# Seven products from the second tile on, earlier sums of weights on GpSimd, and two copies on ScalarE, in a fused attention and feed-forward kernel

## Chip, cores and metric

One core of one Trainium2 chip. The metric is the device time of one execution in microseconds (us); "span" is the time from the first to the last instruction in the trace of one execution, and is about 1.8 us shorter. All runs compared here are of the fast state (single runs without a group are marked so); lower is better.

## What the kernel computes

Attention with keys and values pooled by 8, then a feed-forward layer with the gate `h * cos(h)`:

```python
# q, k, v: (8, 8, 576, 64) float32;  w_in: (512, 2048);  w_out: (2048, 512)
k_p = k.reshape(B, H, Sp, 8, D).mean(axis=3)
v_p = v.reshape(B, H, Sp, 8, D).mean(axis=3)
scores = q @ k_p.T / sqrt(D)
attn = softmax(scores)
x = (attn @ v_p) -> (4608, 512)          # tokens x heads*D
h = x @ w_in
out = (h * cos(h)) @ w_out               # float32
```

The 4608 tokens are cut into nine tiles of 512. Per tile: the *up projection* (64 matmuls of 512 columns, in eight steps of eight; each step ends in a cosine on ScalarE and a product on VectorE, and the products make up `g`), then the *down projection*. Between these matmuls the attention of the next batch is done: scores, exponentials, values, normalisation. GpSimd sums keys and values of the batch after that ("pooling").

## The kernel before: what the change touches

The down projection has two forms. The plain one has 64 matmuls of 512 columns. The other is a 2x2 block product in Winograd's form with seven block products in place of eight: 7 x 16 matmuls of 256 columns. It needs sums of blocks of `g` (`g1` to `g4`, per tile) and of `w_out` (`w2` to `w4`, once). The kernel before uses it from the third tile on (`FIRST = 2`); the sum that product 3 needs is written over half of `w_out` itself, which is only possible after the last plain tile.

```python
FIRST = 2
def put_weights(i, eng, k=None):              # w3, w2, w4: halves of the block sums
    ...
def put_first_weights(i):                     # in place, after tile 1
    w = w_out_sb[i]
    nc.vector.tensor_tensor(out=w[:, :, HM:], in0=w[:, :, HM:], in1=w[:, :, 0:HM], op=SUB)

def put_g12(i): ...                           # VectorE: g1 and g2, half i
def put_g3(i): ...                            # VectorE: g3, half i
def put_g4(i): ...                            # VectorE: g4, half i

for t in range(NT):                           # tiles
    for n, fp in enumerate(up_order(t)):      # eight steps of the up projection
        up_mm(t, fp, ...)                     # matmuls
        up_g(t, fp, ...)                      # cosine on ScalarE, product on VectorE
        if t >= FIRST and 3 <= n < 6:
            (put_g12, put_g3, put_g4)[n - 3](0)
        if t == 1 and 3 <= n < 6:
            put_weights(1, nc.vector, n - 3)
    ...
    if t < FIRST:
        ...                                   # plain down projection with attention between
        if t + 1 == FIRST:
            for i in range(2): put_first_weights(i)
    else:
        product(0); scores_of(u0, u1, u2)     # u2 needs the bank of the eighth up step
        product(1)
        put_g12(1); reads[0](); put_g3(1); reads[1](); put_g4(1)   # reads[0]: the p1 copy
        values(u0); product(2); reads[2](); muls()
        values(u1); product(3); reads[3](); muls()
        values(u2); product(4); reads[4](); muls()
        scores_of(ur, u3)                     # u3 needs the bank that u1's muls() frees
        product(5, ...); ...; product(6); reads[6]()
    ...
    load_kv(b + 1, "k"); load_q(b + 1); load_kv(b + 1, "v")        # loads issued by GpSimd
    if t == 0: put_weights(0, nc.gpsimd)
    pool_add(b + 1, "k"); pool_add(b + 1, "v")                     # GpSimd
```

The softmax here doesn't subtract the row's maximum and nothing guards it: scores larger than these inputs give would overflow.

## Time and profile before

| | kernel before |
|---|---|
| median of 3 runs | 294.95 us (294.61 to 295.21) |
| profiled execution | 296.27 us, span 294.5 us |
| TensorE busy | 96% of the span, granted clock 0.999 |
| tile 0 (down part), 1, 2, 3 | 19.37, 31.60, 31.90, 29.93 us |
| tiles 7 and 8 with the end | 27.46 and 31.30 us |

A tile is counted from its first up matmul to that of the next. The lines for tiles 1 to 3 are quoted in the prediction; those for tiles 7 and 8 have the same columns (stretch and its length, busy time of TensorE, weight loads, VectorE, ScalarE and GpSimd, granted clock, DMA share, GB/s):

```profile
235.74:263.20 27.46, 26.70 (x193) 17.55 (x193) 21.44 (x28) 14.82 (x17) 0.00 (x0) 1.00 0.17 39
263.20:294.50 31.30, 26.42 (x176) 17.11 (x175) 20.38 (x32) 8.96 (x9) 0.00 (x0) 0.99 0.30 68
```

### The profile page before, as it was taken

Reading aid. Unit: us, or ns where it says so; the run is one execution under the profiler, and the core shown is the slowest. Engines: PE = TensorE matmul, PEld = TensorE weight load, DVE = VectorE, ACT = ScalarE, POOL = GpSimd, SP = SyncE. Lnnn points to the kernel's source line nnn. Section 1 sums busy time; section 2 is a strip of 40 time slices with the busy share of each in tenths; the row PEclk is TensorE's granted clock in tenths of the full one; section 3 lists DMA queues with packets and bytes.
Section 4 is the critical chain, followed back from the end, with each engine's and each line's share of the span. In section 5 each row is a group of like instructions: output and inputs, shape, how many; then the busy total and the mean of one; then the engine's idle time right before and its main releaser. Section 6 shows DMA issues by size and latency. Waiting matters only on the chain. (4 is left out here: it accounts for less than half of the span.)

```text
span 294.5 us, 5317 instructions
## 1 busy us (share of the span) xinstructions
PE 282.1 (96%) x2096; PEld 174.0 (59%) x2120; DVE 226.6 (77%) x306; ACT 206.4 (70%) x261; POOL 148.4 (50%) x144
## 2 busy tenths in 40 slices
PE   8899999999999899999999999999999999999984
PEld 3545544444544587458745874588458844774673
DVE  5558547595489998799879887998798879846972
ACT  3786897469767688679967997699769976336500
POOL 8563079993995299536983599349900000000000
PEclk9999999999999999999999999999999999999999
DMA  7999999629817961969185929691840060005014
GB/s 163 205 207 206 207 205 204 139 52 148 168 37 137 139 104 26 200 89 163 19 182 89 169 45 195 92 174 28 173 73 2 4 142 0 2 21 122 2 36 107
DMA packets 44488, 32.95 MB, mean 112 GB/s; under 512 B 22192, under 2 KB 40112, under 8 KB 44464
## 3 DMA queue, kind: packets, MB, share of 16 engines
q0 software_dynamic: 19744, 18.07, 39.2%
q1 hardware_dynamic: 24080, 14.03, 22.2%
q10 hardware_dynamic: 640, 0.52, 0.7%
q8 instruction: 16, 0.26, 0.3%
q14 instruction: 8, 0.07, 0.1%
HBM read 36.70 MB, written 9.44 MB: 157 GB/s over the span
## 5 line engine op out<-in xcount | busy, mean ns | idle before, releaser
L317 PE MATMUL bank<-xT,w_in_sb 128*128 128x512 bf16 x503 | 114.7, 379 | 1.8 <-DVE g_sb L331 0.9
L327 ACT ACTIVATE cos<-bank,half_pi 128x1024 f32<-128x1024 f32 x65 | 71.4, 1113 | 48.5 <-PE bank L317 45.2
L317 PEld LDWEIGHTS <-w_in_sb 128*128 128x128 bf16 x576 | 56.0, 98 | 67.2 <-issue 1.5
L331 DVE TENSOR_TENSOR g_sb<-bank,cos 128x1024 bf16<-128x1024 f32 x65 | 78.4, 1220 | 22.1 <-ACT cos L327 22.0
L151 POOL TENSOR_TENSOR half_sums<-kv_st 72x512 f32<-72x512 bf16 x48 | 56.9, 1212 | 27.3 <-DMA kv_st<-in_k_dram 26.8
L262 DVE TENSOR_TENSOR xT<-bank,inv 64x512 bf16<-64x512 f32 (+1 forms) x72 | 45.3, 629 | 17.9 <-ACT inv L258 16.9
L257 ACT ACTIVATE inv<-bank 64x512 f32<-64x512 f32 (+1 forms) x72 | 39.1, 544 | 12.4 <-PE bank L251 11.2
L402 PEld LDWEIGHTS <-g 128*128 128x128 bf16 x448 | 42.9, 98 | 8.2 <-issue 3.3
L229 ACT ACTIVATE ex<-bank 72x1024 bf16<-72x1024 f32 (+1 forms) x40 | 35.1, 928 | 3.2 <-PE bank L222 3.0
L402 PEld LDWEIGHTS <-g_sb 128*128 128x128 bf16 x336 | 32.1, 98 | 6.9 <-issue 1.0
L153 POOL TENSOR_TENSOR half_sums<-half_sums 72x512 f32<-72x512 f32 x24 | 30.4, 1284 | 0.0
L334 PE MATMUL obank<-w_out_sb,g_sb 128*128 128x512 bf16 x123 | 29.9, 379 | 0.3 <-issue 0.2
L402 PE MATMUL obank<-w,g 128*128 128x256 bf16 x224 | 26.9, 272 | 1.7 <-DVE p_sb L416 1.6
L402 PE MATMUL obank<-w_out_sb,g_sb 128*128 128x256 bf16 x208 | 25.1, 273 | 0.3 <-DVE g_sb L331 0.3
L402 PE MATMUL obank<-w_out_sb,g 128*128 128x256 bf16 x192 | 24.8, 273 | 0.0
L258 ACT ACTIVATE inv<-inv 128x512 f32<-128x512 f32 (+1 forms) x36 | 21.0, 583 | 1.1
L251 PE MATMUL bank<-ex,vz 72*128 72x256 bf16 (+1 forms) x176 | 20.0, 243 | 0.0
L334 PEld LDWEIGHTS <-g_sb 128*128 128x128 bf16 x128 | 11.8, 97 | 12.5 <-issue 1.0
L251 PEld LDWEIGHTS <-vz 72*128 72x128 bf16 x176 | 13.7, 97 | 4.4 <-DVE xT L262 0.5
L156 POOL TENSOR_TENSOR kp<-half_sums 72x512 bf16<-72x512 f32 x12 | 15.0, 1270 | 0.5
L222 PE MATMUL bank<-qT,kk 64*72 64x256 bf16 (+1 forms) x192 | 13.2, 251 | 1.5 <-DVE g_sb L331 0.6
L402 PE MATMUL obank<-w,g_sb 128*128 128x256 bf16 x112 | 13.4, 273 | 0.0
(83 smaller groups left out, 253.6 us busy)
## 6 DMA issues: line engine op xcount, KB each, us to landing
out_dram<-o_two SPq DMA_DIRECT2D x64, 128.0 KB, 2.4
kv_st<-in_v_dram POOLq DMA_DIRECT2D x8, 576.0 KB, 13.6
kv_st<-in_k_dram POOLq DMA_DIRECT2D x7, 576.0 KB, 7.8
q_b<-in_q_dram POOLq DMA_DIRECT2D x6, 576.0 KB, 9.9
w_in_sb<-in_moe_w_in_dram POOLq DMA_DIRECT2D x4, 512.0 KB, 13.1
w_out_sb<-in_moe_w_out_dram POOLq DMA_DIRECT2D x4, 512.0 KB, 18.5
q_b<-in_q_dram POOLq DMA_DIRECT2D x4, 288.0 KB, 11.7
g_sb<-in_k_dram SPq DMA_DIRECT2D x1, 576.0 KB, 3.7
```

Source lines behind the costliest of these rows:

```text
L151: add(out=s[:, h:h + 2], in0=x[:, h:h + 2, 0:4, :], in1=x[:, h:h + 2, 4:8, :], op=ADD)
L153: add(out=s[:, h:h + 4, 0:2, :], in0=s[:, h:h + 4, 0:2, :], in1=s[:, h:h + 4, 2:4, :], op=ADD)
L229: nc.scalar.activation(out=ex[:, 0:nh * n].rearrange("p (a n) -> p a n", a=2), in_=pair[:Sp, :, 0:nh * n // 2], func=ACTF.Exp, scale=scale ...
L251: nc.tensor.matmul(pair[:, hp, (i // 2) * n:(i // 2 + 1) * n], lhsT=vz[b % 2][:, pj, 2 * hp:2 * hp + 2, :].rearrange("p a d -> p (a d)"), ...
L257: nc.scalar.activation(out=inv[half[1 - hp]], in_=pair[half[1 - hp], hp, 0:w], func=ACTF.Ln)
L258: nc.scalar.activation(out=inv, in_=inv, func=ACTF.Exp, scale=-1.0)
L262: nc.vector.tensor_mul(out=x_out(b, u, half[hp]), in0=cols(pair[half[hp], hp, :], u), in1=cols(inv[half[1 - hp]], u))
L317: nc.tensor.matmul(h[j] if h is obanks else h[:, j, :], lhsT=w_in_sb[fc // 4][:, ki, (fc % 4) * 128:(fc % 4 + 1) * 128], rhs=xT[:, ki, t * ...
L327: nc.scalar.activation(out=c, in_=ps, func=ACTF.Sin, bias=half_pi[:, :1])
L331: nc.vector.tensor_mul(out=o, in0=ps, in1=c)
L334: nc.tensor.matmul(o, lhsT=g_sb[:, fc, ms * 128:(ms + 1) * 128], rhs=w_out_sb[fc // 4][:, fc % 4, :], start=(fc == 0), stop=(fc == FFCH - 1))
L402: mms.append(lambda bank=bank, first=first, g=g, w=w, fc=fc, p=p: nc.tensor.matmul(bank[p], lhsT=g(fc, p), rhs=w(fc), start=(first and fc ...
```

## The change

Its intent: gain the eighth product in tile 1 as well. The block sums must then exist before tile 1's down projection, so `w1` gets its own buffer (paid for by one `o_two` buffer), GpSimd makes four half sums ahead of pooling, VectorE four in tile 0, and of the four pieces of `w_out` (0 to 3) the first of the second row block, piece 2, is loaded one place earlier. In tile 1 the sums of `g` are issued later than elsewhere. In the last two tiles the p1 copy goes to ScalarE.

```diff
-    FIRST = 2
+    FIRST = 1
-    w2, w3, w4 = [... for k in range(2, 5)]
+    w1, w2, w3, w4 = [... for k in range(1, 5)]
-        o = msb.tile([128, 2, d_model], FP32, name="o_two", tag="o_two", bufs=3)[:, 0]
+        o = msb.tile([128, 2, d_model], FP32, name="o_two", tag="o_two", bufs=2)[:, 0]
-    def put_first_weights(i): ...                       # removed
+    def put_weights(i, eng, ks=(1, 3, 2, 4)):           # w1 = b12 - b11 is new
-            (Bb, True, part(g1), of(w_out_sb[0:2], 1)),
+            (Bb, True, part(g1), of(w1)),
-                    nc.vector.tensor_copy(out=out[:, p, m], in_=ps)
+                    (nc.scalar.copy if t >= B - 1 else nc.vector.tensor_copy)(out=out[:, p, m], in_=ps)
-    for cg in range(1, 4):
+    for cg in (2, 1, 3):
         load_w_out(cg)
-            if t >= FIRST and 3 <= n < 6:
+            if t == 1 and n == 6:
+                put_g12(0)
+            if t > 1 and 3 <= n < 6:
                 (put_g12, put_g3, put_g4)[n - 3](0)
-            if t == 1 and 3 <= n < 6:
-                put_weights(1, nc.vector, n - 3)
-            mms = [... for cg in range(4) ...]           # tile 0
+            mms = [... for cg in (0, 2, 1, 3) ...]
... (the plain form of tile 1 with its attention is removed)
+                if n == 4:                               # tile 0, matmul number
+                    put_weights(0, nc.vector, (1,))
+                elif n == 36:
+                    put_weights(1, nc.vector, (3,))
+            put_weights(1, nc.vector, (2, 4))
-            put_g3(1)
+            for i in range(0 if t == 1 else 1, 2):
+                put_g3(i)
             reads[1]()
-            put_g4(1)
+            for i in range(0 if t == 1 else 1, 2):
+                put_g4(i)
-                put_weights(0, nc.gpsimd)
+                put_weights(0, nc.gpsimd, (3, 2, 4))
+                put_weights(1, nc.gpsimd, (1,))
```

More of the change, by code (lines that the diff above doesn't have):

```diff
@@ L71 @@
     g1, g2, g3, g4 = [wpool.tile([128, HF, HT], BF16, name=f"g{i}") for i in range(1, 5)]
-    w2, w3, w4 = [[wpool.tile([128, 4, HM], BF16, name=f"w{k}{i}") for i in range(2)] for k in range(2, 5)]
+    w1, w2, w3, w4 = [[wpool.tile([128, 4, HM], BF16, name=f"w{k}{i}") for i in range(2)] for k in range(1, 5)]
     SpA = -(-Sp // 16) * 16
@@ L343, in down_out @@
             nc.sync.dma_start(out=rows_of[b_, ORDER[pos]], in_=o[rows])
-    def put_weights(i, eng, k=None):
-        vec = eng.tensor_tensor
+    def put_weights(i, eng, ks=(1, 3, 2, 4)):
         (b11, b12), (b21, b22) = [(w[:, :, 0:HM], w[:, :, HM:]) for w in (w_out_sb[i], w_out_sb[i + 2])]
-        for n, (w, x, y, op) in enumerate(((w3, b22, b12, SUB), (w2, w3[i], b11, ADD), (w4, b21, w2[i], SUB))):
-            if k in (None, n):
-                vec(out=w[i], in0=x, in1=y, op=op)
-    def put_first_weights(i):
-        w = w_out_sb[i]
-        nc.vector.tensor_tensor(out=w[:, :, HM:], in0=w[:, :, HM:], in1=w[:, :, 0:HM], op=SUB)
+        for k in ks:
+            out, x, y, op = {1: (w1, b12, b11, SUB), 3: (w3, b22, b12, SUB), 2: (w2, w3[i], b11, ADD),
+                             4: (w4, b21, w2[i], SUB)}[k]
+            eng.tensor_tensor(out=out[i], in0=x, in1=y, op=op)
     def g_part(f, t, f0, f1):
@@ L407, in down_products @@
         p1, v16, q15 = [msb.tile([128, 2, HM], FP32, name=n, tag=n, bufs=1) for n in ("p1_sb", "v_sb", "q_sb")]
-        o1, o2 = [msb.tile([128, 2, d_model], FP32, name="o_two", tag="o_two", bufs=3) for _ in range(2)]
+        o1, o2 = [msb.tile([128, 2, d_model], FP32, name="o_two", tag="o_two", bufs=2) for _ in range(2)]
         m1, m2 = slice(0, HM), slice(HM, d_model)
@@ L560 @@
         if t == 0:
-            mms = [(ms, fc) for hm in range(2) for cg in range(4) for ms in range(2 * hm, 2 * hm + 2)
+            mms = [(ms, fc) for hm in range(2) for cg in (0, 2, 1, 3) for ms in range(2 * hm, 2 * hm + 2)
                    for fc in range(4 * cg, 4 * cg + 4)]
@@ L580 @@
                         (32, lambda: later.pop()()), (32, V_(2, 2)), (40, V_(3, 0))]
-        elif t < FIRST:
-            us = BY_TOKENS
-            def scores_of(*parts):
-                def go():
-                    for f in scores_mm, scores_exp:
-                        for b_, u, bank in parts:
-                            f(b_, u, banks[bank])
-                return go
-            fill = [(4, scores_of((b, us[0], 2), (b, us[1], 0))), (14, V_(0, 1, later)), (16, lambda: later.pop()()),
-                    (19, V_(1, 2)), (35, scores_of((b, us[2], 0), (b, us[3], 1), (t, REST, 2))),
-                    (38, V_(2, 0)), (43, lambda: values(t, REST, banks[1])), (46, V_(3, 2))]
         if t < FIRST:
@@ L603 @@
                     down_out(t, ms, obanks[ms % 2])
-            if t + 1 == FIRST:
-                for i in range(2):
-                    put_first_weights(i)
+                if n == 4:
[3 more added lines that the diff above has]
+            put_weights(1, nc.vector, (2, 4))
         else:
```

## The prediction

> **What bounds the kernel now.** I read the page first, then the timelines of TensorE, VectorE, GpSimd and ScalarE, cut at the starts of the nine tiles of 512 tokens, then the busy times by stretch. The page says who fills the span:
>
> ```profile
> span 294.5 us, 5317 instructions
> PE 282.1 (96%) x2096; PEld 174.0 (59%) x2120; DVE 226.6 (77%) x306; ACT 206.4 (70%) x261; POOL 148.4 (50%) x144
> ```
>
> TensorE (PE) is busy 96% of the time at a granted clock of 0.999. So a change pays only if it takes away work of TensorE or one of its few gaps. The table by stretch (TensorE, weight loads, VectorE, ScalarE, GpSimd) shows tile 1, tile 2 and tile 3, cut where each tile's first up-projection matmul starts:
>
> ```profile
> 52.52:84.12 31.60, 31.21 (x175) 15.14 (x177) 19.14 (x24) 23.21 (x30) 26.23 (x24) 1.00 0.64 115
> 84.12:116.02 31.90, 30.23 (x223) 19.63 (x224) 30.52 (x37) 23.93 (x31) 23.05 (x21) 1.00 0.58 97
> 116.02:145.95 29.93, 29.67 (x224) 19.68 (x224) 25.93 (x34) 24.10 (x32) 19.18 (x18) 1.00 0.70 121
> ```
>
> Tile 3 (29.93 us) is the steady form with seven products; tiles 4 to 6 repeat it to 0.01 us. Tile 1 takes 1.67 us more with TensorE full: it has more matmul work. Tile 2 takes 1.97 us more at the steady amount of work: it waits. TensorE's timeline names the gaps of tile 2, and the two near the end, in tiles 7 and 8:
>
> ```profile
> 97.32 1.89 PE L317 MATMUL bank<-xT,w_in_sb 128*128 128x512 bf16 x8 [0.93 <-DVE g_sb L331]
> 100.79 0.61 PE L402 MATMUL obank<-w_out_sb,g_sb 128*128 128x256 bf16 x4 [0.27 <-DVE g_sb L331]
> 104.81 1.91 PE L402 MATMUL obank<-w,g 128*128 128x256 bf16 x16 [0.19 <-DVE p_sb L416]
> 254.23 1.91 PE L402 MATMUL obank<-w,g 128*128 128x256 bf16 x16 [0.66 <-DVE p_sb L416]
> 281.42 2.13 PE L402 MATMUL obank<-w,g 128*128 128x256 bf16 x16 [0.75 <-DVE p_sb L416]
> ```
>
> In each case TensorE waits for VectorE (DVE). VectorE is late in tile 2 because two subtractions of weights stand ahead of the tile's first products with the cosine, and they collide with GpSimd's pooling:
>
> ```profile
> 86.39 3.49 DVE L355 TENSOR_TENSOR w_out_sb<-w_out_sb 128x1024 bf16<-128x1024 bf16 x2
> 89.81 3.67 DVE L331 TENSOR_TENSOR g_sb<-bank,cos 128x1024 bf16<-128x1024 f32 x3
> 86.38 2.96 POOL L153 TENSOR_TENSOR half_sums<-half_sums 72x512 f32<-72x512 f32 x2
> 76.82 2.48 POOL L153 TENSOR_TENSOR half_sums<-half_sums 72x512 f32<-72x512 f32 x2
> ```
>
> The reader sees two subtractions taking 3.49 us (1.75 each; the same shape alone takes 0.68), and a GpSimd pair stretched from 2.48 to 2.96 us in the same stretch.
>
> **What the Trainium skill says.** (1) "SBUF — State Buffer", section "Who interferes with whom": a VectorE tensor_tensor with both inputs in SBUF contends with GpSimd's reads, and the one that issues second blocks for the whole instruction of the other. The trace agrees: 1.75 against 0.68 us. This bears on every moved weight sum. (2) "TensorE: Matmul & The Clock Gate", section "Back-to-back issue gap": its warm formula, columns over 2.4 plus 2.5 ns, gives 215.8 ns for 512 columns and 109.2 for 256. The trace agrees with the formula: eight matmuls of 512 are 1.73 us apart (216.6 each) and 16 of 256 are 1.75 apart (255.97 to 257.72). It contradicts the 131 ns that the section gives for a sustained stream of 512. (3) "ScalarE: Activation LUTs", section "Table sets: the hidden batching unit": copy lies in every table set. The trace agrees as far as it goes: ScalarE's qT copies between cosines in tile 0 bring no table load.
>
> **The change part by part.**
>
> *Tile 1 with seven products.* It removes 64 matmuls of 512 columns, 64 x 0.2166 = 13.86 us, and adds 7 x 16 of 256 columns, 7 x 1.747 = 12.23 us: minus 1.63 us of TensorE work, which agrees with 31.60 - 29.93 = 1.67. That is the most tile 1 can give. Against it stands a new order on VectorE. The first half of the sums of g (line of put_g12) is issued after the seventh of eight cosine products, in front of the eighth; the first halves of g3 and g4 move into the down projection. The eighth product frees bank 0, and the third block of scores of the next batch waits for bank 0 in program order before product 1. In the steady tile:
>
> ```profile
> 129.84 1.91 PE L402 MATMUL obank<-w_out_sb,g_sb 128*128 128x256 bf16 x16
> 132.46 0.41 PE L222 MATMUL bank<-qT,kk 64*72 64x256 bf16 x4 [0.16 <-DVE g_sb L331]
> 131.19 1.22 DVE L331 TENSOR_TENSOR g_sb<-bank,cos 128x1024 bf16<-128x1024 f32 x1 [0.16 <-ACT cos L327]
> ```
>
> Call the start of product 0 T: there T = 129.84 and the eighth cosine product ends at T + 2.57. For tile 1, T would be 66.37 (where its down projection starts now, as the up projection keeps its work). ScalarE's seventh and eighth cosines start at 64.84 and 66.57 and take 1.11, so the seventh product can run 65.98 to 67.12; the two sums of g take 1.34 (132.44 to 133.78); the eighth runs 68.46 to 69.70 = T + 3.33. So the scores start about 0.76 us later than in tile 3. The same walk on gives the second g sums until 71.04, the p1 copy until 71.64, two g3 pieces until 72.84, the o1 read until 73.44, two g4 pieces until 74.64, the v read, one normalisation, the q read and the next normalisation until about 78.95, where TensorE wants that bank at 78.85: another 0.1 to 0.2. So 0.9 of the 1.65 us is given back: tile 1 gains 0.7 us.
>
> *Tile 2 without the in-place subtractions.* They are removed (w1 has its own buffer). VectorE starts the tile as in tile 3, so the 1.97 us should go. What remains is GpSimd's pooling, late against the tile (below), which may block the first g sums: I give back 0.35 and count 1.6 us.
>
> *Weight sums in tile 0.* GpSimd gets one more, 2.12 us by its row:
>
> ```profile
> 39.65 2.12 POOL L351 TENSOR_TENSOR w<-w_out_sb,w_out_sb 128x1024 bf16<-128x1024 bf16 x1 [1.56 <-DMA w_out_sb<-in_moe_w_out_dram]
> 46.14 4.48 POOL L151 TENSOR_TENSOR half_sums<-kv_st 72x512 f32<-72x512 bf16 x4
> ```
>
> The new load order brings the second operand (the third piece of w_out) one place earlier, which takes away up to the 1.56 us of waiting, so pooling starts 2.2 - 1.55 = 0.65 us later. Three of VectorE's four sums (in tile 0 at the 37th matmul, and two after the last) collide with pooling: by the 0.5 us that the pair above lost, 1.5 in all. Pooling of batch 2 then ends near 66.4 in place of 64.3, its values are read near 71, and the loads for batch 3 go out 2 us later. This is beside TensorE, not on its path: keys are transposed at the third up step of tile 2, when GpSimd's key part is done (estimate 84.4). VectorE's own four sums fall into gaps: 1.34 us idle before 37.06, 0.99 before 49.43, and 3.04 before 56.46 hold 0.68, 1.25 and twice 0.68. Tile 0: 0.0, at worst 0.3 us lost. The plain down projection of tile 0 takes pieces 0, 2, 1, 3 in the order that they now land: nothing.
>
> *Copies on ScalarE in tiles 7 and 8.* Only the p1 copy (obank to p1_sb) moves. VectorE does it after the last g sums; ScalarE is free then:
>
> ```profile
> 252.18 0.59 ACT L229 ACTIVATE ex<-bank 72x512 bf16<-72x512 f32 x1
> 260.34 0.77 ACT L257 ACTIVATE inv<-bank 64x256 f32<-64x256 f32 x2 [7.57 <-PE bank L251]
> 252.88 0.69 DVE L364 TENSOR_TENSOR g<-g,g_sb 128x1024 bf16<-128x1024 bf16 x1
> ```
>
> In tile 7 product 0 is out at about 251.8, the copy (estimate 0.6 us, as ScalarE's 128x512 qT copy took 0.58) runs 252.8 to 253.4, and product 2 then waits only for g2, done at 253.57: it starts near 253.6 in place of 254.23, minus 0.6. In tile 8 ScalarE is idle from 278.3; product 2 starts behind g2 at about 281.0 and loses its inner stall too (its 16 matmuls span 1.97 now, 281.42 to 283.39, against 1.75), minus 0.6. The chain of waits of the page runs from that copy through product 2 to the end, so both count in full: 1.2 us.
>
> *Sum:* 0.7 + 1.6 + 1.2 = 3.5 us. 294.95 - 3.5 = **291.5 us**, 1.2% less. The o_two buffers going from three to two cost nothing: each is written again a tile or 8 us later, and its transfer lands in 2.4 us.
>
> **The rivals.** (a) *All gaps close:* tile 1 falls to 29.95, tile 2 to 29.93. For it: the author deferred sums in tile 1 to keep VectorE free, and VectorE is busy for only 19.14 us of tile 1 now. Against it: the eighth product stands behind two sums in one queue. It would give 1.65 + 1.97 + 1.2 = 4.8, 290.1 us. (b) *VectorE becomes the bound of tile 1,* by GpSimd's blocking: if pooling of batch 2 ends after 67, the two sums in front of the eighth product wait for it, each by up to a GpSimd instruction (about 0.6 to 1.1 us, as w_out_sb's subtractions did). Then tile 1 loses 1 to 2 us more and tile 2 about 0.5: 293.0 to 294.0. For it: an estimated margin of 0.7 us only. (c) *Tile 2's wait is merely replaced:* pooling of batch 3 starts later (estimate 75, in place of 72.4) and still runs at the first g sums of tile 2 (92.5); half of the 1.97 stays: 292.4.
>
> **Range and chances.** The end's 1.2 us is firm (0.9 to 1.3), tile 2 gives 1.0 to 2.0, tile 1 minus 0.6 to plus 1.6, tile 0 costs 0 to 0.3. Rival (a) bounds the low side near 290.1, (b) the high side near 294. The range is 290.3 to 293.1. Faster by over 2% needs 289.05, below even (a): chance 0.02. Slower by over 2% needs a new stall of 9 us: 0.01.
>
> **What would show it right or wrong.** In the profile after: tile 1 near 30.9 us with a gap of about 0.9 us at its scores behind the eighth cosine product; tile 2 near 30.3 without the gaps of 0.93 and 0.27; the gaps of 0.66 and 0.75 before product 2 below 0.15; GpSimd's first pooling near 46.8 and its value sums of batch 2 done by 66.5; no new table load. A gap in tile 0, a wait for w1 or w2, or a scores wait for kk of batch 2 or 3 would make the prediction wrong.

## The result and the profile after

The changed kernel took 293.69 us in the median of 4 runs (293.17 to 294.17) against 294.93 of 4 runs before. The ratio is 0.9958, with a 95% interval of 0.9934 to 0.9982. Ratios here are the mean time of one kernel's fast runs over that of the other's of the same rounds, so not quite the ratio of the medians. The result is correct. The class (within 2%) was forecast, but the time lies above my range of 290.3 to 293.1: I forecast a gain of 3.5 us, and it is 1.2.

The table by stretch of the changed kernel (columns as before): tile 0 from the start of its down projection, tiles 1 and 2, then 7 and 8.

```profile
33.06:53.30 20.24, 19.49 (x131) 9.32 (x130) 12.53 (x18) 16.44 (x23) 15.96 (x11) 1.00 1.11 197
53.30:85.54 32.24, 29.95 (x226) 19.80 (x225) 28.79 (x35) 23.04 (x30) 26.78 (x24) 1.00 0.57 96
85.54:115.47 29.93, 29.77 (x227) 19.68 (x224) 25.58 (x34) 24.11 (x32) 19.17 (x19) 1.00 0.75 121
235.59:262.23 26.64, 26.64 (x194) 17.56 (x192) 20.82 (x27) 15.30 (x18) 0.00 (x0) 1.00 0.18 40
262.23:292.40 30.17, 26.21 (x178) 17.09 (x175) 19.71 (x30) 9.60 (x11) 0.00 (x0) 0.97 0.31 71
```

TensorE's work in tile 1 did fall (31.21 to 29.95 us busy; 31.44 in a later trace of the kernel before, b_trace2), yet the tile grew from 31.60 to 32.24: the saved matmul time came back as waiting, and more. Tile 2 is now exactly a steady tile. Tiles 7 and 8 lost 0.82 and 1.13 us. TensorE's timeline names the waits:

```profile
37.91 0.81 PE L334 MATMUL obank<-w_out_sb,g_sb 128*128 128x512 bf16 x3 [0.70 <-DMA w_out_sb<-in_moe_w_out_dram]
70.47 0.41 PE L222 MATMUL bank<-qT,kk 64*72 64x256 bf16 x4 [0.89 <-DVE g_sb L331]
81.01 0.41 PE L222 MATMUL bank<-qT,kk 64*72 64x256 bf16 x4 [1.40 <-DVE xT L262]
171.21 0.41 PE L222 MATMUL bank<-qT,kk 64*72 64x256 bf16 x4 [0.29 <-DVE xT L262]
```

The 0.89 is the gap that the prediction announced behind the eighth cosine product. The 1.40 at the scores of `u3` was announced as 0.1 to 0.2. The 0.29 lies in tile 4, which took 30.33 us here and 29.93 in the second trace of this kernel (a_again), so it is chance. VectorE's and GpSimd's timelines of tile 1 show why:

```profile
72.39 1.28 DVE L364 TENSOR_TENSOR g<-g_sb 128x1024 bf16<-128x1024 bf16 x2
73.59 0.68 DVE L414 TENSOR_TENSOR o_two<-obank,p_sb 128x512 f32<-128x512 f32 x1
74.19 2.60 DVE L368 TENSOR_TENSOR g<-g_sb,g 128x1024 bf16<-128x1024 bf16 x2
76.72 0.68 DVE L414 TENSOR_TENSOR v_sb<-obank,p_sb 128x512 f32<-128x512 f32 x1
...
73.33 5.59 POOL L151 TENSOR_TENSOR half_sums<-kv_st 72x512 f32<-72x512 bf16 x4 [5.07 <-DMA kv_st<-in_k_dram]
```

Two `g3` pieces take 1.28 us while GpSimd waits for keys. The two `g4` pieces, of the same shape, take 2.60 once GpSimd pools batch 3 (from 73.33); GpSimd's four sums stretch as well, from 4.48 to 5.59. Everything behind on VectorE's queue is late by 1.3 us, down to the normalisation that frees the bank of `u3`.

The end is better than forecast. VectorE and ScalarE in tile 7:

```profile
252.53 0.57 ACT L412 COPY p_sb<-obank 128x512 f32<-128x512 f32 x1
252.74 0.69 DVE L360 TENSOR_TENSOR g<-g,g_sb 128x1024 bf16<-128x1024 bf16 x1
253.26 5.40 PE L398 MATMUL obank<-w,g 128*128 128x256 bf16 x48
```

Product 2 starts at 253.26, right behind product 1, though the second piece of `g2` is only done near 253.4: its first matmuls read the first piece. There was only one wait there, the copy, and it is gone. ScalarE's table loads are 18 in both kernels, which agrees with the Trainium skill ("ScalarE: Activation LUTs", section "Table sets: the hidden batching unit") that copy is in every table set.

### The profile page after: what moved, and what is told of

Same layout as the page of the kernel before. It is cut to its first block, busy times and chain, and to the rows that moved or that the text cites. A ratio compares the mean times of both kernels' runs of the same rounds, so it can differ in the third digit from the quotient of the medians.

```text
span 292.4 us, 5446 instructions
## 1 busy us (share of the span) xinstructions
PE 280.6 (96%) x2168; PEld 178.1 (61%) x2168; DVE 232.4 (79%) x314; ACT 208.1 (71%) x265; POOL 149.9 (51%) x145
## 5 line engine op out<-in xcount | busy, mean ns | idle before, releaser
L327 ACT ACTIVATE cos<-bank,half_pi 128x1024 f32<-128x1024 f32 x64 | 70.3, 1113 | 46.9 <-PE bank L317 46.3
L331 DVE TENSOR_TENSOR g_sb<-bank,cos 128x1024 bf16<-128x1024 f32 x64 | 77.3, 1220 | 22.5 <-ACT cos L327 22.4
L398 PEld LDWEIGHTS <-g 128*128 128x128 bf16 x512 | 49.0, 98 | 6.9 <-issue 1.2
L398 PE MATMUL obank<-w,g 128*128 128x256 bf16 x368 | 43.6, 273 | 0.0
L398 PEld LDWEIGHTS <-g_sb 128*128 128x128 bf16 x384 | 36.8, 98 | 7.3 <-issue 1.2
L398 PE MATMUL obank<-w_out_sb,g_sb 128*128 128x256 bf16 x240 | 28.7, 273 | 0.0
L334 PE MATMUL obank<-w_out_sb,g_sb 128*128 128x512 bf16 x64 | 15.7, 380 | 0.7 <-DMA w_out_sb<-in_moe_w_out_dram 0.7
L398 PE MATMUL obank<-w_out_sb,g 128*128 128x256 bf16 x112 | 15.6, 273 | 0.0
L398 PE MATMUL obank<-w,g_sb 128*128 128x256 bf16 x128 | 15.3, 273 | 0.0
L317 PE MATMUL obank<-xT,w_in_sb 128*128 128x512 bf16 x64 | 15.1, 379 | 0.0
```

The lines of the kernel that those rows point to most:

```text
L317: nc.tensor.matmul(h[j] if h is obanks else h[:, j, :], lhsT=w_in_sb[fc // 4][:, ki, (fc % 4) * 128:(fc % 4 + 1) * 128], rhs=xT[:, ki, t * ...
L327: nc.scalar.activation(out=c, in_=ps, func=ACTF.Sin, bias=half_pi[:, :1])
L331: nc.vector.tensor_mul(out=o, in0=ps, in1=c)
L398: mms.append(lambda bank=bank, first=first, g=g, w=w, fc=fc, p=p: nc.tensor.matmul(bank[p], lhsT=g(fc, p), rhs=w(fc), start=(first and fc ...
```

## The experiments

Theory after the result: (1) the end gives 1.95 us; (2) tile 2 gave little in a usual run, because my trace was of an unusual one; (3) tile 1 loses by the blocked `g4` sums. Rivals: the copies are worth only the 1.2 us forecast and the rest lies elsewhere; tile 2 is always slow and some other part lost the gain; tile 1's second gap comes from the order on VectorE's queue alone. Medians and ratios to the kernel before in the same rounds:

| run | us | ratio | tile 1 / tile 2 in its trace |
|---|---|---|---|
| b_again (before) | 296.38 | 1.0021 | 31.70 / 31.86 |
| b_copies | 293.21 | 0.9918 | 31.70 / 30.30 |
| a_nocopies | 296.26 | 1.0019 | 31.88 / 29.93 |
| a_again (after) | 293.74 | 0.9934 | 32.25 / 29.94 |
| c_plain1 | 293.25 | 0.9921 | 31.29 / 30.49 |
| a_oldorder | 293.09 | 0.9911 | 31.14 / 30.42 |
| a_late_g4 | 292.69 | 0.9899 | 31.26 / 29.93 |
| a_late_g4_n5 | 291.57 | 0.9874 | 30.35 / 29.94 |

**The kernel before again: b_again, b_trace2, b_trace3** (no edit).

> The kernel before, unchanged, for a second trace. The first one was taken in a run of 296.27 us, 1.3 us above the median of 294.93, so a part of what I read as removable may be peculiar to that run. Theory A (the two in-place subtractions of weights collide with GpSimd's pooling by chance): tile 2 takes about 30.6 in place of 31.90 us here and the subtractions about 2.2 in place of 3.49 us. Rival B (tile 2 always takes about 31.9, and the first trace was slow elsewhere or is a mere offset of the whole): tile 2 takes 31.7 to 32.1. Time 294.9 either way.

> The kernel before once more, for a third trace. Its runs fall into two groups, near 295 (most) and near 296.5 to 297 (few); both traces so far come from the upper group (296.27 and 296.99) and have tile 2 at 31.9 us. Theory: the groups are two states of tile 2, which differ by about 1.6 us; a run near 295 shows tile 2 at about 30.3 us and the pair of subtractions at 2.5 us, one near 296.5 shows 31.9 and 3.4 to 3.5. Rival: tile 2 is 31.9 in a run near 295 too, and the extra time of the upper group lies elsewhere.

> The kernel before, for a fourth trace; the same expectation as for the third: tile 2 at 30.3 if the run is near 295, at 31.9 if it is near 296.5.

Measured: b_again's profiled run (296.99 us) has tile 2 at 31.86 us; so far that spoke for the rival. Its time missed the forecast of 294.9: three of its six runs lie at 295.43 to 295.90, three at 296.85 to 296.99. b_trace2 (one run, 294.55 us) has 30.24, b_trace3 (one run, 295.98) 30.19. In b_trace2 the stretches of tiles 1 and 2 and the two subtractions with GpSimd beside them read:

```profile
52.58:84.02 31.44, 31.44 (x178) 15.10 (x176) 19.08 (x24) 23.21 (x30) 25.96 (x24) 1.00 0.65 116
84.02:114.26 30.24, 30.13 (x225) 19.61 (x224) 28.86 (x37) 23.72 (x31) 21.48 (x20) 1.00 0.62 102
...
86.30 2.39 DVE L355 TENSOR_TENSOR w_out_sb<-w_out_sb 128x1024 bf16<-128x1024 bf16 x2
86.42 3.38 POOL L153 TENSOR_TENSOR half_sums<-half_sums 72x512 f32<-72x512 f32 x2
```

In the first trace VectorE's pair took 3.49 and GpSimd's 2.96. Here the pair takes 2.39 and GpSimd's 3.38. Who waits for whom is settled by who starts first, and by little: where GpSimd's pair started 0.01 or 0.05 us before VectorE's (the first trace and b_again), VectorE's took 3.49 and 3.44; where VectorE's started 0.12 to 0.22 us ahead (b_trace2, b_trace3, b_copies), it took 2.38 to 2.49. TensorE's tile 2 is 31.9 us in the first case and 30.2 or 30.3 in the second. So tile 2 has two states. That 30.2 is the usual one is an inference from the times: it fits the runs near 295, which are the most (9 of the 12 runs of before in the first set of rounds and all 11 in the second lay at 294.87 to 295.95). The expectation for b_trace3 was incomplete: at 295.98 its tile 2 is the short one, and the rest is a longer tile 0 (20.16 us in its down part against 19.38, with two waits for pieces of `w_out`, 0.24 and 0.22) and a longer tile 1 (31.78 against 31.44, with a wait of 0.32 for a product of VectorE). Such waits for `w_out` occur with both kernels: the down part of tile 0 takes 19.37 to 20.16 in the four traces of before, 20.24 and 20.07 in the two of the change, and 19.38 to 19.47 in three traces of a_nocopies, whose tile 0 is the same code. The gap of 0.70 us in the first trace of the change is therefore nothing that the change must bring; whether it brings it more often is not shown.

**Copies alone, and all but the copies: b_copies, a_nocopies, a_nocopies2, a_nocopies3, a_again.**

```diff
 # b_copies: the kernel before with this line of the change; a_nocopies: the change without it
-                    nc.vector.tensor_copy(out=out[:, p, m], in_=ps)
+                    (nc.scalar.copy if t >= B - 1 else nc.vector.tensor_copy)(out=out[:, p, m], in_=ps)
```

> The kernel before with only the p1 copies of the last two tiles moved to ScalarE. From the traces (tile 7 27.46 to 26.64, tile 8 31.30 to 30.17 us) the theory is minus 1.95 us: near 293.0. My prediction's reading (TensorE would still wait for g2) gives minus 1.2: 293.7. A rival under which the copies only move the wait gives 294.9.

> The changed kernel with the p1 copies of the last two tiles back on VectorE. If the copies are worth 1.95 us here as well and the rest of the change has lost time: 295.6, slower than before. If they are worth 1.2: 294.9. If the gain came from tiles 1 and 2 instead: 293.7.

> The changed kernel again, for a second trace. Theory: the gap of 0.70 us in tile 0 that waits for a piece of w_out varies with the start-up transfers (the four runs of this kernel lie at 293.2 to 293.3 and 294.1 to 294.2), so here it is either near 0 or near 0.7. The gap of 1.40 us in tile 1 at the scores behind the second normalisation comes again, within 0.3 us, as do two g4 pieces of 2.6 us in sum. Rival: the 1.40 us is chance and falls below 0.7. Time 293.7.

Measured: in the traces tile 7 is 26.64 with the copies on ScalarE and 27.46 without, in every trace of either kernel, and tile 8 differs by 1.1; that is the 1.95 us. The copies alone give 293.21 us, no worse than the whole change (293.74 in the same rounds), and the change without them gives 296.26, no better than before. So the copies made the whole gain; the rest of the change gained nothing and, by a_again against b_copies, lost about 0.5 us. a_again repeats the gap of 0.89, the one of 1.40 (1.41), and tile 1 at 32.25. By medians the copies are worth 2.5 to 3.2 us, more than the traces show, because the runs of both kernels with VectorE's copies spread upward in these rounds (a_nocopies: 294.65 to 297.23). Two more traces of a_nocopies were to show where:

> The changed kernel with VectorE's copies at the end, for a second trace. Its six runs lay between 294.65 (the traced one) and 297.23, while the kernels with ScalarE's copies stay within 1.1 us. Theory: the upper runs are waits in tiles 0 and 1 (0.7 and 0.4 us more, as in two traces of the changed kernel), so the trace of a run near 296 shows tile 0 at 21.8 to 22.0 and tile 1 at 32.2. Rival: something behind tile 6 takes longer in these runs, and tiles 7 and 8 together take over 58.9 us (58.8 in the first trace).

> The same kernel for a third trace, with the same expectation: above 296 either tiles 0 and 1 are the longer ones (theory) or tiles 7 and 8 (rival).

They came out at 294.96 and 295.21 us (one run each), with tiles 0 and 1 short and tiles 7 and 8 as in the first trace, so no slow run was caught. What made a_nocopies take 295.7 to 297.2 us in five of its six runs stays open; I count the copies at the traced 1.95. It isn't the two states of tile 2, since this kernel has no subtractions in place and its tile 2 is 29.93 us in all three traces; so not every upper run of the kernel before need be one with a long tile 2 either. These runs were on another of the two chips than the two later traces, but the chip alone is not it either: a_nopool3 below, with ScalarE's copies and on the second chip, spread from 293.75 to 297.29.

These three traces show something else that changes the reading of tile 1. Up to tile 6 they run the changed kernel's code, without its wait for `w_out` in tile 0. There the collision is smaller: the pair of `g4` takes 2.24 us in place of 2.60, the second gap is 1.10 or 1.11 in place of 1.40, and tile 1 takes 31.88 or 31.89 in place of 32.24. From a_nocopies:

```profile
73.46 2.24 DVE L368 TENSOR_TENSOR g<-g_sb,g 128x1024 bf16<-128x1024 bf16 x2
79.92 0.41 PE L222 MATMUL bank<-qT,kk 64*72 64x256 bf16 x4 [1.10 <-DVE xT L262]
```

So about 0.35 us of tile 1's 32.24 goes with the late tile 0 of both traces of the change.

**The seven products of tile 1: c_plain1.** The changed kernel, but with `FIRST = 2` and the plain tile 1 back; own `w1`, early sums, load order and copies stay.

```diff
-    FIRST = 1
+    FIRST = 2
+        elif t < FIRST: ...            # plain tile 1 with its attention, as before
-                if n == 4:
+                if t == 0 and n == 4:  # and likewise for the other early sums
-            if t == 1 and n == 6:
-                put_g12(0)
```

> The changed kernel in all (own buffers and early sums of weights, new load order, copies on ScalarE), but tile 1 keeps its plain down projection. It tells what the seven products in tile 1 alone are worth. Theory (they lose: 1.65 us less matmul work against gaps of 0.89 and 1.40 us): tile 1 goes from 32.24 back to about 31.65, tile 2 stays at 29.93, time 293.1, some 0.6 below the changed kernel. Rival (my prediction: they gain 0.7): 294.4.

Measured: 293.25 us, tile 1 at 31.29, tile 2 at 30.49. The theory said 293.1, the rival 294.4. The time came out, but not by the tiles forecast (31.65 and 29.93): tile 1 is shorter and tile 2 longer. In the form chosen, the seven products of tile 1 cost about 0.5 us by the medians and 0.4 by tiles 1 and 2 together (62.17 in the first trace of the change against 61.78); against the a_nocopies traces, where the two tiles take 61.81 or 61.82, they cost nothing. Either way they don't gain. And c_plain1 against b_copies (0.9921 and 0.9918) says that the earlier sums of weights on their own are worth nothing in a usual run.

**GpSimd's part in the 1.40 us: a_nopool3 and a_nopool3b.** Both give a wrong result.

```diff
 # a_nopool3: the first two of three stages left out for batch 3
-        for h in range(0, H, 2):
+        for h in range(0, 0 if b == 3 else H, 2):
 # a_nopool3b: all stages left out
-            pool_add(b + 1, "k")
-            pool_add(b + 1, "v")
+            if b + 1 != 3:
+                pool_add(b + 1, "k")
+                pool_add(b + 1, "v")
```

> The changed kernel without GpSimd's first two stages of sums for batch 3 (a wrong result on purpose), so that GpSimd does not read SBUF beside VectorE's g3 and g4 pieces of tile 1. Theory (the blocking stretches the two g4 pieces from 1.2 to 2.6 us, and that makes the gap of 1.40 at the scores): the pair takes 1.2 to 1.3, the gap falls to 0.1 to 0.2, tile 1 takes 31.0 us, the time is near 292.5. Rival (the gap is made by the order on VectorE's queue alone): the gap stays above 1 us. The gap of 0.89 behind the eighth cosine product stays in both.

> The changed kernel without any GpSimd sums for batch 3 (a wrong result on purpose). The first form kept the last stage of these sums, which then ran early and blocked the sums of g before the eighth cosine product (a gap of 2.54 us). Without it the theory is: gap of 0.89 at the third scores as before, two g4 pieces in 1.2 to 1.3 us, gap at the scores of the last block 0.1 to 0.2, tile 1 about 31.0 us. Rival (queue order alone makes the second gap): it stays above 1 us and tile 1 near 32.2.

The first form misfired (294.78 us, four runs). The stage that I had left in no longer waited for the others and ran at 68.73, beside the sums of `g` that stand before the eighth product:

```profile
68.33 2.25 DVE L360 TENSOR_TENSOR g<-g,g_sb 128x1024 bf16<-128x1024 bf16 x1
70.49 1.21 DVE L331 TENSOR_TENSOR g_sb<-bank,cos 128x1024 bf16<-128x1024 f32 x1
68.73 2.96 POOL L156 TENSOR_TENSOR kp<-half_sums 72x512 bf16<-72x512 f32 x2
```

One sum took 2.25 us in place of 0.69, and the gap in front of the scores of `u2` grew from 0.89 to 2.54: the blocking shown in another place. In the clean form the pair of `g4` takes its 1.28 us and the second gap is gone; the first gap stays:

```profile
73.71 1.28 DVE L368 TENSOR_TENSOR g<-g_sb,g 128x1024 bf16<-128x1024 bf16 x2
```

Tile 1 takes 30.92 us (expected 31.0) and the run 292.29 (two runs). So GpSimd's reading is the cause of the second gap, 1.3 us of tile 1's 32.24 (1.0 of the 31.88 in a_nocopies, which like this run had no wait in tile 0). The rival, queue order alone, falls: the order is the same here.

**The order of the pieces of `w_out`: a_oldorder.**

```diff
-    for cg in (2, 1, 3):
+    for cg in range(1, 4):
-            mms = [... for cg in (0, 2, 1, 3) ...]
+            mms = [... for cg in range(4) ...]
```

> The changed kernel with the pieces of w_out loaded and used in the order 0, 1, 2, 3 again. Theory: GpSimd waits for piece 2 again before its first weight sum (1.5 to 2.3 us in the traces of the kernel before), so pooling of batch 2 starts at about 48.3 and ends near 67.5, when the sums of g before the eighth cosine product run: they are blocked, and the gap of 0.89 grows by 0.5 to 1 us: 294.3 to 294.7. Rival: the order is worth nothing: 293.7.

Both the theory and the rival missed: 293.09 us, below the change. GpSimd does start later, and the first gap does grow, from 0.89 to 1.11 only. But pooling of batch 3 then starts at 76.64, after the `g4` sums:

```profile
74.67 1.28 DVE L368 TENSOR_TENSOR g<-g_sb,g 128x1024 bf16<-128x1024 bf16 x2
76.64 4.50 POOL L151 TENSOR_TENSOR half_sums<-kv_st 72x512 f32<-72x512 bf16 x4 [5.15 <-DMA kv_st<-in_k_dram]
```

Tile 1 is 31.14. Tile 2 pays 0.5 us of it back (30.42; its pooling now ends later). The new load order made GpSimd earlier, and just thereby led it into the collision.

**Moving the sums of `g` in tile 1: a_late_g4 and a_late_g4_n5.**

```diff
 # a_late_g4: the second g4 piece behind the normalisation that u3's scores wait for
             reads[1]()
-            for i in range(0 if t == 1 else 1, 2):
-                put_g4(i)
+            put_g4(0 if t == 1 else 1)
 ...
             product(3); reads[3](); muls()
+            if t == 1:
+                put_g4(1)
 # a_late_g4_n5: besides
-            if t == 1 and n == 6:
+            if t == 1 and n == 5:
                 put_g12(0)
```

> The changed kernel with the second g4 piece of tile 1 issued behind the normalisation that the scores wait for. Theory: the gap of 1.40 falls to about 0.2, tile 1 takes 31.1, time 292.6. Rival: product 5 then waits for g4 instead, by about 0.5 to 1.3 us, and the time is 293.3 to 293.7.

> The run a_late_g4 with, besides, the first two sums of g of tile 1 one step earlier (after the sixth cosine product, not the seventh). Theory: the gap of 0.89 behind the eighth cosine product falls to about 0.3 since the sums then use VectorE's pauses of 0.5 us, tile 1 takes 30.5, time 292.0. Rival: these sums collide with GpSimd's last value sums of batch 2 (until 65.7) and the gap stays, time 292.6.

a_late_g4: 292.69 us, tile 1 at 31.26, the second gap 0.49 (expected 0.2: the piece left in place still took 1.63). No wait of product 5 for `g4` is in the trace, so the rival falls. Tile 0 had no wait here; like with like, against the 31.88 of a_nocopies, the move gained 0.6 us. a_late_g4_n5: 291.57 us, tile 1 at 30.35. One gap of note is left:

```profile
68.59 0.61 PE L398 MATMUL obank<-w_out_sb,g_sb 128*128 128x256 bf16 x4 [0.45 <-DVE g_sb L331]
```

This is the fastest kernel and correct: 0.9874 of the kernel before (0.9856 to 0.9892), and below the change by 1.8 us by the ratios, 2.1 by the medians. In it the seven products of tile 1 gain 0.9 us against c_plain1's plain tile (and tile 2 is 0.55 shorter). The `o_two` buffers were not tested alone; no trace shows a wait for one.

## Why the prediction was wrong, by its own steps

- **Tile 2, "the 1.97 us should go".** The mechanism was right: tile 2 is a steady tile now, 29.93 us. The size was wrong. I took the state of one trace as the kernel's usual one, although that execution took 296.27 us against a median of 294.95. In a usual run tile 2 took 30.2, so 0.3 us was there to gain, not 1.6. This term is short by 1.3 us.
- **Tile 1, "so 0.9 of the 1.65 us is given back: tile 1 gains 0.7 us".** The gap behind the eighth cosine product came as worked out (0.89). The step that failed is "two g4 pieces until 74.64", which counted 0.6 us each. VectorE's order was walked rightly: counted from the start of tile 1, the pieces began at 20.89 us, forecast 20.92. What failed is the start of GpSimd's pooling of batch 3, which I had estimated at 75, behind them; it started at 73.33, on top of them, and they took 2.60. I had let its loads go out 2 us later than before. They went out 0.87 later, and the pooling began 0.96 later. Before, then after:

```profile
64.92 0.86 POOL L114 DMA_DIRECT2D kv_st<-in_k_dram  x1
72.37 4.48 POOL L151 TENSOR_TENSOR half_sums<-kv_st 72x512 f32<-72x512 bf16 x4 [4.98 <-DMA kv_st<-in_k_dram]
...
65.79 0.86 POOL L114 DMA_DIRECT2D kv_st<-in_k_dram  x1
```

Tile 1 lost 0.64 against the first trace and 0.8 against b_trace2, or 0.44 in the traces of a_nocopies without the wait in tile 0. The term, forecast at a gain of 0.7, is off by 1.1 to 1.5 us, and with it the sign of the change's main idea. Rival (b), VectorE as the bound of tile 1 by GpSimd's blocking, was the right one, but I set it at the first sums and it struck at `g4`; its 293.0 to 294.0 held the time, in part by luck, as it knew neither of the tile 2 error nor of the one at the end.
- **The end, "product 2 then waits only for g2".** Forecast 1.2, measured 1.95. Product 2 begins on the first piece of `g2`, so the copy was the only wait. This term is 0.75 us too small, and it hid part of the other two errors.
- **Tile 0, "0.0".** I had named a gap in tile 0 as a sign of being wrong, and both traces of the change have one for `w_out` (0.70 and 0.53). Most of this variation (0.8 of 0.9 us) occurs in the kernel before too, and three traces of a_nocopies with the same tile 0 have none, so it isn't counted against the sum; tile 1 was the worse in the runs that had it.
- The sum with the terms as measured against b_trace2: 0.3 for tile 2, minus 0.8 for tile 1, 1.95 for the end, 1.45 us (1.8 with the 0.44 of tile 1), where the runs show 1.2 (medians of the first rounds) to 1.9 (second).
- Slips of the working that changed little: 1.73 us for eight matmuls is 216.3 ns each, not 216.6. Rival (c) counted the 0.35 us given back a second time: half of tile 2's wait staying gives 292.1, not 292.4. And the terms' own ranges add up to a gain of 1.0 to 4.9 us, so to 293.95 at the slow end; the range stopped at 293.1.

## What to carry to other kernels

Before working out a gain from a trace, compare the time of the traced execution with the median: where it is off by as much as the gain, take further traces first, because a wait that depends on the phase of two engines can have two sizes. Where VectorE's sums and GpSimd's both read SBUF, don't count on the length that an instruction has alone (a pair of `g4` here: 1.28 us alone, 2.24 or 2.60 beside GpSimd); making GpSimd earlier is not always better. The saved matmuls paid only after VectorE's instructions were placed anew: two moves in tile 1 turned nothing gained, or a loss of up to 0.5 us, into a gain of 1.5 us in tiles 1 and 2 together (61.78 in c_plain1, 60.29 in a_late_g4_n5). Test the parts of a bundled change alone: here one line made the whole gain.

## What the Trainium skill lacked or had wrong

- "TensorE: Matmul & The Clock Gate", section "Back-to-back issue gap", gives 131 ns for a sustained stream of 512 columns and calls its formula an over-count there. In the traces eight such matmuls with their weight loads take 1.73 us (97.32 to 99.05 in the first trace), 216 ns each, which is the formula.
- "SBUF — State Buffer", section "Who interferes with whom", is right that the two engines block each other (0.69 against up to 2.25 us for one VectorE sum), but says nothing of repeated meetings: beside GpSimd's unbroken sums a pair of VectorE sums took 2.60 in place of 1.28 us and stretched four GpSimd sums from 4.48 to 5.59. Its rule that the order of issue decides who blocks fits the two states of tile 2; what it doesn't say is that this order can flip between executions of one kernel (the same pair 3.49 or 2.39 us).
